# Attention with a gated MLP on one core: the first four pairs' scores from plain fp32 operands, and PSUM banks handed out per use

## The chip, the core and the metric

The kernel runs on one core of a Trainium2 chip. The core has TensorE (PE: matmuls, with a separate path for loading weights, PEld), VectorE (DVE), ScalarE (ACT) and GpSimd (POOL); SyncE (SP) issues all DMAs of this kernel. TensorE writes into PSUM, which the kernel uses as eight banks of 512 fp32 columns. The metric is device time in microseconds of one execution; the profile is of one execution on the chip.

## The reference

There are 8 batches of 8 heads, 576 positions, head size 64. Queries and keys are rotated, scores are softmaxed, values are weighted; the eight heads side by side (512 columns) are the input of a gated MLP with a spatial mix.

```python
q_rot, k_rot = (rotate(q), rotate(k))
scores = scale * np.matmul(q_rot, k_rot.transpose(0, 1, 3, 2))
scores = scores - np.max(scores, axis=-1, keepdims=True)
attn = np.exp(scores)
attn = attn / (np.sum(attn, axis=-1, keepdims=True) + 1e-09)
x = np.matmul(attn, v)                 # heads side by side: (8, 576, 512)
h = np.maximum(x @ w_in, 0.0)          # w_in 512 x 1024
u, v = h[..., :512], h[..., 512:]
v_n = (v - mu) / np.sqrt(var + 1e-06)  # mean and variance over the 512 columns
v_s = np.einsum('ts,bsd->btd', w_spatial, v_n) + b_spatial[None, :, None]
out = (u * v_s) @ w_out                # w_out 512 x 512
```

## The kernel before, in words

**Pairs.** Two heads of a batch form a pair: head 0 in partitions 0 to 63, head 1 in 64 to 127, positions along the columns. There are 32 pairs, numbered through; pairs 0 to 3 are batch 0. A pair's scores are nine tiles of 128 queries by 576 keys: tiles (0,0) to (0,3) of head 0, (1,0) to (1,3) of head 1, and (0,4), the last 64 queries of both heads. A score tile takes a place of two PSUM banks (288 keys in each); names `sc` in the profile.

**Two ways to score.** Pair 0 scores from plain fp32 operands (`mm_whole` in `scores`, L650): a tile of head h takes the 64 rows of that head, two matmuls, and each fp32 matmul stands as two passes in the trace. Pairs 1 to 31 score in fp32r (L641). There the operands are split into a high and a low part, and `prepare` copies them with ten DMAs into stacks of 128 rows (`qs`, `ks`, `lks`, one set for each head): a tile is four matmuls of 128 rows, tile (0,4) six. The split costs two roundings of whole tiles (L449 and L320) and two corners (`qt`) on ACT, one pass on DVE (L425, the low part of q) and one on POOL (L323, `lk`). The rotation itself is POOL's: two products and a sum each for q and k (L433, L437). The stacks exist once, so the next pair's copies wait for the last tile that reads them.

**After a tile.** DVE takes the row maxima (L661, `nmx`), ACT the exponential with its sum (L663, `et`), and then the place is free. In pairs 0 to 3 (`attention_plain`) TensorE transposes the exponentials in groups of three (L533, L536, `tp`), ACT or DVE copies the group out (L542, L544, `turns`), and TensorE multiplies with the values (L573, `pv`). From pair 4 on DVE transposes (L665) and TensorE multiplies in 32-row pieces (L603, `pvl`, `pvu`). `normalise` sends the sums through DRAM (`rt`, `rb`) and multiplies (L694).

**MLP.** Once the four pairs of a batch are normalised, `mlp` runs four sets of products: `pa` (L728), `pb` (L751), `pc` (L769), `pd` (L784). Between them and the pairs of the next batch TensorE alternates. The MLP's weights arrive as raw 64-bit numbers and are decoded once, in twelve blocks of 512 columns (`decode`, six passes on DVE and two on ACT a block, in a PSUM bank of their own).

**What sets the order.** No order is written out. Each step is an `op` with an engine, an assumed duration, a priority key (20 a pair, `K_...` constants as offsets) and what it reads and writes. `Program.run` plays the ops through with these durations: whenever an engine is free it takes the ready op with the lowest key whose buffers it can get, and that fixes each engine's order. The numbers of buffers are in `SLOTS`. In PSUM there are two places for score tiles (`sc`, banks 0 to 3) and four single banks (`pm`) for everything else: transposes, values, decode, MLP.

## Time and profile before

| | |
|---|---|
| median of 3 runs | 881.13 us (874.3, 881.13, 881.17) |
| profiled execution | 876.26 us, its span 874.5 us |
| mean granted clock of TensorE | 0.994 |
| busy: PE, DVE, ACT, POOL | 824.3, 602.2, 517.2, 512.0 us |
| DMA | 150.82 MB, 172 GB/s over the span |
| first score matmul, first MLP product | 9.2 us, 110.4 us |

A row of a group in the profile gives the line, the engine, the operation, output and inputs by name and shape, the count, busy time and mean duration, and the engine's idle time before these instructions with what ended it. A row of the timeline or of the chain begins with the start and the length in us. A row of a window gives for each engine the busy time in it, the granted clock of TensorE and the DMA's share and rate. TensorE's busy time is an upper bound of its work, because matmuls are pipelined.

### The profile page before, as it was taken

The page shows a single profiled execution, that of the slowest core. Times are in us where ns is not written, and L with a number is a line of the kernel's source. Part 1 is how long each engine was busy: PE and PEld are TensorE (multiplying, and loading weights), DVE is VectorE, ACT ScalarE, POOL GpSimd, SP SyncE. Part 2 cuts the span into 40 slices and gives each one's busy share as a digit, 9 for nine tenths or more (in the row PEclk, how much of TensorE's full clock was granted, in tenths as well). Part 3 has the DMA queues.
Part 4 walks back from the last instruction along what each step waited for, and adds up shares of the span by engine and source line. Part 5 has one row for each costly group of instructions (what it writes and reads, how often), then busy time and mean ns, then how long its engine had stood idle before and what let it go on. Part 6 is the DMA issues. An engine that isn't in the chain of part 4 may idle for free.

```text
span 874.5 us, 30219 instructions
## 1 busy us (share of the span) xinstructions
PE 824.3 (94%) x12554; PEld 744.4 (85%) x12554; DVE 602.2 (69%) x1213; ACT 517.2 (59%) x1303; POOL 512.0 (59%) x433
## 2 busy tenths in 40 slices
PE   4988899899999999998999999998999989999998
PEld 2665578789899998898899998988899978999898
DVE  4688989686787767666787657766687648875230
ACT  2788768455675557554676547645576536754342
POOL 6577755673586657574477754675486735742221
PEclk9999989999999999999999999999999999999999
DMA  6767787757677786668877786668677667663101
GB/s 238 231 198 201 200 243 169 165 141 208 178 193 192 175 206 169 162 170 202 200 180 178 170 207 182 174 168 209 172 186 191 161 173 203 166 142 91 48 1 55
DMA packets 68171, 150.82 MB, mean 172 GB/s; under 512 B 14530, under 2 KB 14786, under 8 KB 68035
## 3 DMA queue, kind: packets, MB, share of 16 engines
q1 hardware_dynamic: 68034, 148.90, 65.8%
q8 instruction: 99, 1.62, 0.8%
q14 instruction: 38, 0.30, 0.1%
HBM read 93.55 MB, written 9.58 MB: 118 GB/s over the span
## 4 chain that ended last, share of the span: by engine, by line
PE 59%; POOL 12%; DVE 9%; DMA 8%; ACT 7%; issue 3%; SPq 1%; POOLq 0%; ACTq 0%; DVEq 0%
PE sc L641 10%; PE pa L728 9%; PE pvu L603 9%; PE pd L784 8%; PE pc L769 8%; PE pvl L603 6%; DMA qs<-st 5%; PE pb L751 4%; POOL st L433 3%; DVE nmx L661 3%; POOL lk L323 2%; ACT et L663 2%; PE pv L573 2%; POOL st L437 2%; POOL x L323 2%
## 5 line engine op out<-in xcount | busy, mean ns | idle before, releaser
L661 DVE TENSOR_REDUCE nmx<-sc 128x1 f32<-128x576 f32 x288 | 212.4, 746 | 121.6 <-PE sc L641 110.1
L663 ACT ACTIVATE et<-sc,nmx 128x576 f32<-128x576 f32 x288 | 212.0, 737 | 115.1 <-DVE nmx L661 114.4
L433 POOL TENSOR_TENSOR st<-st,tabs 128x576 f32<-128x576 f32 x124 | 175.4, 1432 | 111.0 <-DMA st<-in_qk_dram 66.2
L665 DVE STREAM_TRANSPOSE et<-et 128x576 f32<-128x576 f32 x252 | 191.5, 766 | 38.0 <-ACT et L663 36.2
L603 PE MATMUL pvl<-et,vr 32*64 32x160 f32 (+1 forms) x4032 | 155.3, 294 | 9.1 <-issue 6.3
L603 PEld LDWEIGHTS pvl<-et,vr 32*64 32x64 f32 x4032 | 137.7, 131 | 22.4 <-issue 16.9
L603 PE MATMUL pvu<-et,vr 32*64 32x128 f32 (+1 forms) x4032 | 152.8, 294 | 3.6 <-issue 2.6
L641 PE MATMUL sc<-ks,qs 128*128 128x288 f32 x620 | 135.1, 307 | 18.1 <-ACT et L663 8.8
L641 PEld LDWEIGHTS sc<-ks,qs 128*128 128x128 f32 x620 | 98.1, 188 | 38.7 <-ACT et L663 14.1
L603 PEld LDWEIGHTS pvu<-et,vr 32*64 32x64 f32 x4032 | 122.2, 130 | 5.2 <-issue 3.5
L769 PE MATMUL pc<-wsp,vn 128*128 128x288 f32 x768 | 121.3, 295 | 0.0
L784 PE MATMUL pd<-g,wo 128*128 128x288 f32 x768 | 119.2, 299 | 0.0
L728 PE MATMUL pa<-wi,x 128*128 128x512 f32 x448 | 118.7, 402 | 0.4 <-DVE wi L323 0.3
L751 PE MATMUL pb<-x,wi 128*128 128x288 f32 x768 | 117.2, 296 | 0.6 <-DVE x L621 0.6
L751 PEld LDWEIGHTS pb<-x,wi 128*128 128x128 f32 x768 | 107.7, 188 | 3.6 <-issue 1.2
L784 PEld LDWEIGHTS pd<-g,wo 128*128 128x128 f32 x768 | 107.8, 190 | 2.5 <-issue 2.5
L769 PEld LDWEIGHTS pc<-wsp,vn 128*128 128x128 f32 x768 | 108.6, 188 | 0.3 <-DVE dcwo L364 0.2
L641 PE MATMUL sc<-lks,qs 128*128 128x288 f32 x496 | 106.2, 296 | 0.0
L728 PEld LDWEIGHTS pa<-wi,x 128*128 128x128 f32 x448 | 81.9, 192 | 16.2 <-issue 1.3
L323 POOL TENSOR_TENSOR vn<-vv,vn 128x512 fp32r<-128x512 f32 x32 | 41.2, 1290 | 88.6 <-ACT vn L320 84.8
L437 POOL TENSOR_TENSOR st<-st 128x576 f32<-128x576 f32 x62 | 89.2, 1439 | 3.8
L323 POOL TENSOR_TENSOR g<-u,g 128x288 fp32r<-128x288 f32 x64 | 54.2, 854 | 62.7 <-ACT g L320 62.7
(149 smaller groups left out, 1053.2 us busy)
## 6 DMA issues: line engine op xcount, KB each, us to landing
vr<-in_v_dram SPq DMA_DIRECT2D x116, 320.0 KB
st<-in_qk_dram SPq DMA_DIRECT2D x64, 576.0 KB
qs<-st SPq DMA_DIRECT2D x124, 144.0 KB
ks<-st SPq DMA_DIRECT2D x124, 144.0 KB
lks<-lk SPq DMA_DIRECT2D x62, 144.0 KB
out_dram<-ob SPq DMA_DIRECT2D x31, 288.0 KB
ws<-in_w_spT_dram SPq DMA_DIRECT2D x2, 576.0 KB
tabs<-in_tab_dram SPq DMA_DIRECT2D x1, 576.0 KB
```

The lines of the kernel that those rows point to most:

```text
L323: eng.tensor_tensor(out=lo, in0=src, in1=hi.bitcast(F32), op=ALU.subtract)
L433: f = lambda e: e.tensor_tensor(out=st[j][:, cols], in0=st[j][:, cols], in1=tabs[:, cols], op=ALU.mult)
L437: f = lambda e: e.tensor_tensor(out=st[j][:, :S], in0=st[j][:, :S], in1=st[j][:, S:2 * S], op=ALU.add)
L603: nc.tensor.matmul(bank(g)[64 * h:64 * h + 64, c0:c0 + 32 * (s1 - s0)], lhsT=vr[rows, b % 4, b // 4, h, :], rhs=et[rows, s0:s1, 32 * b:32 ...
L641: nc.tensor.matmul(pt[:, c * 512:c * 512 + HALF], lhsT=lhsT, rhs=rhs[:, c * HALF:(c + 1) * HALF], start=(n == 0), stop=(n == len(parts) - 1))
L661: op(DVE, 720, key + K_MAX, lambda: nc.vector.tensor_reduce(out=nmx.tile, in_=tops(), op=ALU.max, axis=AX.XY, negate=True), r=[pt], w=[nmx ...
L663: op(ACT, 880, key + K_EXP, lambda: nc.scalar.activation(et[:, at, :].rearrange("p (c n) -> p c n", c=2), tops(), AF.Exp, bias=nmx.tile, s ...
L665: op(DVE, 740, key + K_TURN, lambda: nc.vector.transpose(out=et[:, at, :], in_=et[:, at, :]), w=[(et, at)])
L728: nc.tensor.matmul(pm.tile, lhsT=lhsT, rhs=win[1, d][:, j, :], start=(d == 0 and n == 0), stop=(d == 3 and n == len(todo) - 1))
L751: nc.tensor.matmul(pm[:, :HALF], lhsT=win[0, d][:, i, f * P:(f + 1) * P], rhs=x[d][:, at:at + HALF], start=(d == 0 and n == 0), stop=(d == ...
L769: nc.tensor.matmul(pm[:, :HALF], lhsT=lhsT, rhs=rhs, start=(t == 0 and n == 0), stop=(t == 4 and n == 1))
L784: nc.tensor.matmul(pm[:, :HALF], lhsT=wout[d,][:, i, m * P:(m + 1) * P], rhs=gs[d][:, at:at + HALF], start=(d == 0 and n == 0), stop=(d == ...
```

## The change: what it does

1. Pairs 0 to 3 (`WHOLE` 1 to 4) score from plain fp32. `prepare_whole` for pairs 1 to 3: load, rotate and sum on POOL, one scaling of q by 1/8 on ACT; no split, no stacks.
2. `scores_whole` is one step for two tiles, t of head 0 and t of head 1: its matmuls go by half of the keys, and in each half head 0 and then head 1, in the two halves of the rows. It needs two score places at once (one for tile (0,4)). `RESERVE` keeps such a step's claim on places while it waits for them.
3. PSUM is one tile of eight banks. Banks are given out per use: a score tile takes two neighbouring banks from the bottom, within a limit of 4 tiles in pair 0, 3 in pairs 1 to 3, 2 later (`SCORE_SLOTS`, `limit`); single banks come from the top, 7 down to 4.
4. The stacks are opened late (`open_stacks`): their memory holds operands of pairs 0 and 1 first, and their zero fills run on POOL after pair 1 has scored.
5. A group of transposes waits only for the head whose exponentials it reads. Eight of the twelve weight decodes start only after the scores of pair 2, 3 or 4 (`GATE_U`, `GATE_O`).
6. Assumed durations are changed (DMAs with a rate of the wire, exponential 880 to 750 ns, maximum 720 to 680, decode 640 to 605), and the keys. `mlp(0)` is listed after pair 4 in place of pair 3.

```diff
-MOE_START, MOE_LENGTH = 90, 82
+MOE_START, MOE_LENGTH = 91.9, 82.99
...
-K_MAX, K_EXP, K_TURN, K_AV, K_COPY = 1.0, 2.0, 3.0, 24.0, 4.0
+K_MAX, K_EXP, K_TURN, K_AV, K_COPY = 1.55, 3.4, 2.08, 20.54, -3.71
...
-WHOLE = 1
+WHOLE = 4
+HOMES = [("stk", "stk"), ("stk", "stage"), ("stage", "stage"), ("xg", "xg")]
+RESERVE = True
+SCORE_SLOTS = [4, 3, 3, 3]
...
+        def vacant(pool, limit):
+            if pool not in PSUM:
+                return free[pool][0] if free[pool] else None
+            if pool == "pm":
+                return next((n for n in range(7, 3, -1) if banks[n] is None), None)
+            return next((n for n in range(limit) if banks[2 * n] is banks[2 * n + 1] is None), None)
...
+        opened = [t for a in range(2) for t in (("qs", a, 0), ("qs", a, 1), ("ks", a, 0), ("ks", a, 1), ("lks", a))]
+        op(POOL, 1800, 20 * WHOLE - 25, place, r=[("scored", i) for i in range(min(WHOLE, 2))], w=opened, new=wide)
...
+        else:
+            for j, st in ((1, k), (0, q)):
+                op(DMA, dma_ns(576), key - K_LOADW - j, lambda j=j, st=st: load(st.tile, qk[b, hp, j].rearrange("p c n -> p (c n)")), w=[(st, 0), (st, 1)], new=[st])
...
+            op(ACT, 573, key - K_HIQ, lambda: nc.scalar.activation(q[:, :S], q[:, :S], AF.Copy, scale=0.125), w=[(q, 0), (q, 1)])
...
+    def scores_whole(i, t, st, sm, et, key, new, turn):
+
+        q, k = st
+        pts = [Buf("sc", None, None, f"sc{i}_{a}_{t}") for a in range(2 if t < 4 else 1)]
+        for pt in pts:
+            pt.limit = SCORE_SLOTS[i]
+
+        def mm():
             for c in range(2):
+                for h in range(2):
                     own = slice(64 * h, 64 * h + 64)
                     q0 = t * P + TW * h if t < 4 else 4 * P * (1 - h)
+                    pt, rows = (pts[h], slice(0, P)) if t < 4 else (pts[0], own)
+                    nc.tensor.matmul(pt[rows, c * 512:c * 512 + HALF], lhsT=q[own, q0:q0 + rows.stop - rows.start], rhs=k[own, c * HALF:(c + 1) * HALF], start=True, stop=True)
...
+        o = op(PE, 1150, key, mm, r=[*need, *([] if new else [(et, "first")])], w=[*pts, *done, *([(et, "first")] if new else [])], new=[*pts, *new])
+        o.reserve = RESERVE
```

How the instructions move is shown at three places of TensorE's order. The first is the program's start. Before, pair 0's tiles of the two heads come one after the other (`sc0_h_t` is tile t of head h), and two groups of transposes stand ahead of the last:

```order
L650 MATMUL sc0_0_0_117<-st0_1_88,st0_0_103 128x288 x2
L650 MATMUL sc0_1_0_121<-st0_1_88,st0_0_103 128x288 x2
L650 MATMUL sc0_0_1_133<-st0_1_88,st0_0_103 128x288 x2
L650 MATMUL sc0_1_1_139<-st0_1_88,st0_0_103 128x288 x2
L650 MATMUL sc0_0_2_151<-st0_1_88,st0_0_103 128x288 x2
L650 MATMUL sc0_1_2_159<-st0_1_88,st0_0_103 128x288 x2
L650 MATMUL sc0_0_3_173<-st0_1_88,st0_0_103 128x288 x2
L650 MATMUL sc0_1_3_185<-st0_1_88,st0_0_103 128x288 x2
L533 MATMUL tp0_0_0a_193<-turns_83,et0_118 128x128 x3
L533 MATMUL tp0_0_0b_200<-turns_83,et0_118 128x128 x3
L650 MATMUL sc0_0_4_204<-st0_1_88,st0_0_103 64x288 x4
```

Now (L727 scores, L593 transposes, L633 values; all write the one PSUM tile):

```order
L727 MATMUL psum_63<-st0_1_83,st0_0_94 128x288 x16
L727 MATMUL psum_63<-st0_1_83,st0_0_94 64x288 x4
L593 MATMUL psum_63<-turns_78,et0_108 128x128 x15
L633 MATMUL psum_63<-turns_78,vr0_96 64x384 x2
L593 MATMUL psum_63<-turns_78,et0_108 128x128 x3
```

All nine tiles of pair 0 now stand ahead of its first transpose. The second place is pair 1's values with pair 2's scores. Before:

```order
L641 MATMUL sc2_1_1_612<-ks1_77,qs1_75 128x288 x2
L641 MATMUL sc2_1_1_612<-lks1_79,qs1_75 128x288 x2
L573 MATMUL pv1_1_578<-turns_83,vr1_128 64x192 x2
L641 MATMUL sc2_0_2_627<-ks0_76,qs0_74 128x288 x2
L641 MATMUL sc2_0_2_627<-lks0_78,qs0_74 128x288 x2
L573 MATMUL pv1_1_578<-turns_83,vr1_128 64x192
```

Now (`st2` is pair 2's operands, four matmuls are two tiles):

```order
L727 MATMUL psum_63<-st2_1_121,st2_0_134 128x288 x4
L593 MATMUL psum_63<-turns_78,et1_219 128x128 x6
L633 MATMUL psum_63<-turns_78,vr1_113 64x384 x2
L593 MATMUL psum_63<-turns_78,et1_219 128x128 x3
L633 MATMUL psum_63<-turns_78,vr1_113 64x192 x4
L593 MATMUL psum_63<-turns_78,et1_219 128x128 x3
L727 MATMUL psum_63<-st2_1_121,st2_0_134 128x288 x4
```

Single tiles among transposes and values have become steps of two tiles with more of the other work between them. The third place is what stands ahead of the first MLP product (L728, now L810). Before:

```order
L573 MATMUL pv3_1_1087<-turns_83,vr3_420 64x128
L641 MATMUL sc4_1_1_1169<-ks1_77,qs1_75 128x288 x2
L641 MATMUL sc4_1_1_1169<-lks1_79,qs1_75 128x288 x2
L641 MATMUL sc4_1_2_1176<-ks1_77,qs1_75 128x288 x2
L641 MATMUL sc4_1_2_1176<-lks1_79,qs1_75 128x288 x2
L641 MATMUL sc4_1_3_1197<-ks1_77,qs1_75 128x288 x2
L641 MATMUL sc4_1_3_1197<-lks1_79,qs1_75 128x288 x2
L728 MATMUL pa0_0_1205<-wi10_284,x0_467 128x512 x3
```

Now (`stk0` holds queries and keys of head 0, `stk1` of head 1, `stk2` the low parts of the keys):

```order
L633 MATMUL psum_63<-turns_78,vr3_344 64x128
L706 MATMUL psum_63<-stk1_453 128x288 x2
L706 MATMUL psum_63<-stk2_454,stk1_453 128x288 x2
L706 MATMUL psum_63<-stk0_452 128x288 x2
L706 MATMUL psum_63<-stk2_454,stk0_452 128x288 x2
L706 MATMUL psum_63<-stk0_452 128x288 x2
L706 MATMUL psum_63<-stk2_454,stk0_452 128x288 x2
L706 MATMUL psum_63<-stk0_452 128x288 x2
L706 MATMUL psum_63<-stk2_454,stk0_452 128x288 x2
L810 MATMUL psum_63<-wi10_325,x0_400 128x512 x6
```

Four tiles stand there in place of three, and three of them belong to pair 5. In the batches that follow, the products and the pairs' steps alternate in much the same way as before.

More of the change, by code (lines that the diff above doesn't have):

```diff
@@ L33 @@
 LATE = 1500
+KIB_NS = 3.6
+AHEAD = 1633
 FETCH = 2500
@@ L152, in place @@
             for b in bufs:
-                pool = next((p for n, p in enumerate(b.pools) if free[p] and not (n and own[p])), None)
+                pool = next((p for n, p in enumerate(b.pools) if vacant(p, b.limit) is not None and not (n and own[p])), None)
                 if pool is None:
                     for t in taken:
-                        free[t.pool].insert(0, t.slot)
+                        occupy(t, None)
                     return False
-                b.pool, b.slot = pool, free[pool].pop(0)
+                b.pool, b.slot = pool, vacant(pool, b.limit)
+                occupy(b, b)
                 taken.append(b)
@@ L641, in mm @@
                     nc.tensor.matmul(pt[:, c * 512:c * 512 + HALF], lhsT=lhsT, rhs=rhs[:, c * HALF:(c + 1) * HALF], start=(n == 0), stop=(n == len(parts) - 1))
-        def mm_whole():
+        heads = [a] if t < 4 else [0, 1]
+        need = [("qs", h, j) for h in heads for j in range(2)] + [("ks", h, j) for h in heads for j in range(2)] + ([("lks", a)] if t < 4 else [lk, "qt"])
+        done = [("scored", i)] if (a, t) == TILES[-1] else []
+        op(PE, 4 * pe_ns(HALF) if t < 4 else 6 * pe_ns(HALF), key, mm, r=[*need, *([] if new else [(et, "first")])], w=[pt, *done, *([(et, "first")] if new else [])], new=[pt, *new])
@@ L660, in scores @@
-        op(PE, 8 * pe_ns(HALF) if i < WHOLE else 4 * pe_ns(HALF) if t < 4 else 6 * pe_ns(HALF), key, mm_whole if i < WHOLE else mm, r=[*need, *([] if new else [(et, "first")])], w=[pt, *([(et, "first")] if new else [])], new=[pt, *new])
-        op(DVE, 720, key + K_MAX, lambda: nc.vector.tensor_reduce(out=nmx.tile, in_=tops(), op=ALU.max, axis=AX.XY, negate=True), r=[pt], w=[nmx], new=[nmx])
+        op(DVE, 680, key + K_MAX, lambda: nc.vector.tensor_reduce(out=nmx.tile, in_=tops(), op=ALU.max, axis=AX.XY, negate=True), r=[pt], w=[nmx], new=[nmx])
```

206 lines of the change are left out of this document (123 added, 83 removed).

## The prediction

> **What bounds the kernel now.** I read the page first (busy shares, slices), then the windows by stage, then the chain and the timeline of the first 110 us, then who waited for whom there.
>
> ```profile
> PE 824.3 (94%) x12554; PEld 744.4 (85%) x12554; DVE 602.2 (69%) x1213; ACT 517.2 (59%) x1303; POOL 512.0 (59%) x433
> ```
>
> TensorE is busy for 94% of the span, so what counts is when it gets work and what that work costs. The windows part the run: the plain stage (28.43 to 110.4; the first MLP product starts at 110.4 us), the first 5 us of the MLP, one MLP batch.
>
> ```profile
> core 0: us, PE busy (x) PEld busy (x) DVE busy (x) ACT busy (x) POOL busy (x), PEclk, DMA share, GB/s
> 28.43:47.30 18.87, 18.87 (x139) 13.02 (x138) 13.04 (x22) 15.79 (x39) 9.41 (x7) 1.00 0.60 201
> 47.30:68.20 20.90, 18.45 (x141) 12.69 (x140) 17.23 (x29) 16.83 (x42) 15.72 (x13) 1.00 0.73 207
> 68.20:88.80 20.60, 18.38 (x135) 11.96 (x135) 16.77 (x30) 17.20 (x43) 15.22 (x12) 1.00 0.75 218
> 88.80:110.40 21.60, 17.79 (x132) 12.30 (x130) 20.80 (x36) 16.88 (x44) 15.31 (x13) 0.96 0.80 193
> sum 81.97, PE 73.48 PEld 49.98 DVE 67.84 ACT 66.71 POOL 55.67; mean PE 18.37 PEld 12.49 DVE 16.96 ACT 16.68 POOL 13.92
> ...
> 110.40:115.40 5.00, 5.00 (x13) 3.94 (x13) 3.49 (x7) 2.32 (x7) 4.71 (x4) 0.51 1.04 273
> ...
> 218.50:317.80 99.30, 97.35 (x1666) 90.73 (x1666) 72.21 (x147) 60.33 (x155) 65.26 (x54) 1.00 0.74 186
> ```
>
> Each pair of the plain stage takes 19 to 22 us, of which TensorE works 18 to 19: it is the bound there, with 81.97 - 73.48 = 8.5 us idle, and DVE is next (20.80 of 21.60 in the last window). An MLP batch takes about 100 us with 2 us of idle. So a saving is worth its face value only if it brings the first MLP product forward, or takes idle time from the batches. Ahead of the plain stage lie the scores of pair 0, told by the chain and by the timeline of TensorE:
>
> ```profile
> 9.16 2.30 PE sc L650 x8
> 11.48 0.77 DVE nmx L661
> 12.29 0.05 issue
> 12.34 0.84 ACT et L663 x2
> 13.18 0.04 issue
> 13.22 2.30 PE sc L650 x6
> ...
> 13.22 3.01 PE L650 MATMUL sc<-st,st 64*128 64x288 f32 x8 [1.77 <-ACT et L663]
> 17.22 3.07 PE L650 MATMUL sc<-st,st 64*128 64x288 f32 x8 [0.99 <-ACT et L663]
> 21.29 3.62 PE L650 MATMUL sc<-st,st 64*128 64x288 f32 x8 [1.00 <-ACT et L663]
> 24.84 0.90 PE L533 MATMUL tp_0a<-turns,et 128*128 128x128 f32 x3
> 25.54 0.84 PE L533 MATMUL tp_0b<-turns,et 128*128 128x128 f32 x3
> 26.31 2.19 PE L650 MATMUL sc<-st,st 64*64 64x288 f32 x8
> ```
>
> Two tiles start together, and the next two wait until the exponentials of these are done and their banks free: a round of 4 us (9.16, 13.22, 17.22, 21.29), of which TensorE works 2.3. The ninth tile ends at 28.5 us.
>
> **The change, part by part.** *Pair 0's scores.* By the order, five operations (two tiles each, the last one tile) now stand ahead of the first transpose, with four tile places. The first two need no place of another: 9.16 + 2.30 = 11.5 us, and about 13.5 us. The third needs the first one's places: exponentials at 12.34 + 0.84 and once more, 14.0 us, so it ends at 16.0. The fourth waits for the exponentials of the second (maxima from 13.5, exponentials done by 16.0) and ends at 18. The fifth, one tile, ends at about 20. The two transposes that stood before the ninth tile (0.90 + 0.84, overlapping: 1.5 us) come after, so that the point reached at 28.5 is reached at 21.5: **-7**. Its bounds: the nine exponentials alone, 12.34 + 9 x 0.84 = 19.9, would allow -8.5; one more wait for a place, 1 us as in the row of 17.22, leaves -6.
>
> By the Trainium skill (TensorE: Matmul & The Clock Gate, What's actually happening) TensorE leaves its half clock after some 3.4 us of sustained work; here the first transposes at 24.84 still ran slow though TensorE had worked with 1 us gaps since 9.16, and with the gaps closed the third to fifth operation would by that rule run at half their time, which makes the sum below about 866 in place of 867.
>
> *The work of pairs 1 to 3.* What a score tile costs stands in the chain, cold and warm:
>
> ```profile
> 24.91 0.83 PE tp_0a L533 x3
> 25.74 0.64 PE tp_0b L533 x3
> ...
> 32.86 0.33 PE tp_3b L533 x3
> ...
> 54.54 0.52 PE sc L641 x4
> ...
> 57.66 0.72 PE sc L641 x4
> ...
> 88.15 0.79 PE sc L641 x6
> ```
>
> The same transposes take 0.64 us early and 0.33 later, so early TensorE runs at half speed and a two-tile operation of 2.30 us should be 1.15 warm. Its two heads already run side by side before: eight passes in 2.30 us (and in 2.19, 64 columns) are four passes' time. A pair then costs 5 x 1.15 = 5.8 us. The stacked form costs 0.52 a tile behind a transpose and 0.72 behind a value product, eight times, and 0.79: 5.0 to 6.6. Equal within a microsecond, three times: 0, from -2.5 to +2.5. The half-row shape differs from that of the transposes, where the stacked tile had the same; counted in the order up to the first MLP product, TensorE changes shape 86 times, 76 before. At 0.72 - 0.52 = 0.2 each that is +2; some fall into idle time: **+1**.
>
> *Waits in the plain stage.* Of its idle time nearly all is one kind:
>
> ```profile
> PE sc L641 <- ACT et L663: 6.3, 6, 1.8
> PE tp L536 <- ACT turns L542: 1.2, 1, 1.2
> PE tp_2a L533 <- DVE turns L544: 0.9, 2, 0.6
> ```
>
> A tile waits for its place. The old order put three to six tiles in a row behind each other; the new one spreads the five operations of a pair over the values of the pair before, though four tiles in a row still stand ahead of the first MLP product. But an operation now takes both places at once. Behind a waiting operation stand all transposes and values of the order, and DVE and ACT wait for those. I take half of the 6.3 us away, **-3**; bounds -6.3 (all goes) and +8 (as much idle again).
>
> *What pairs 1 to 3 no longer need.* Per pair: ten copies of 144 KB, two roundings and two corners on ACT, one pass each on DVE and POOL; one scaling on ACT comes in.
>
> ```profile
> L323 POOL TENSOR_TENSOR lk<-st 128x576 fp32r<-128x576 f32 x31 | 44.3, 1430 | 9.5 <-ACT st L320 8.5 <-ACT et L663 0.4
> L425 DVE SCALAR_TENSOR_TENSOR st<-st 128x576 fp32r<-128x576 f32 x31 | 28.1, 906 | 3.3 <-ACT st L449 3.3
> L449 ACT ACTIVATE st<-st 128x576 fp32r<-128x576 f32 x31 | 21.1, 682 | 12.6 <-POOL st L437 11.2 <-DMA ks<-st 1.4
> L320 ACT ACTIVATE st<-st 128x576 fp32r<-128x576 f32 x31 | 21.0, 676 | 2.6 <-POOL st L437 2.6
> L320 ACT ACTIVATE qt<-st 64x64 fp32r<-64x64 f32 x62 | 15.6, 251 | 2.0 <-PE sc L641 1.6
> ```
>
> POOL loses 3 x 1.43 = 4.3 us, DVE 3 x 0.91 = 2.7, ACT 3 x (0.68 + 2 x 0.25) = 3.5, the queues 30 x 144 KB = 4.3 MB. None of it ends the stage while TensorE has work in front of it: 0; if DVE decides at its end, -2.7. The stacks' fills move from the start to pair 4's preparation on POOL, whose load was 55.67 of 81.97 us: hidden; without that cover some 1 us. The gate on the last eight weight decodes only orders DVE's work; it doesn't change its amount.
>
> *Behind the first product.* The clock of 0.51 in the window from 110.4 costs 5 x 0.49 = 2.4 us. It follows idle time at the end of the stage, and the row of four tiles there is as long: 0, bound -2.4. In the batches the same work stands in nearly the same order with other times; what may change is this wait in 218 to 818 us:
>
> ```profile
> PE sc L641 <- DMA qs<-st: 7.3, 8, 1.7
> ```
>
> I take 0: all of it gone would be -7, as much again +7; for a range half of each is enough, since the copies keep their number and their queue.
>
> Three tiles of pair 5 now stand ahead of the first product, 3 x 0.52 = 1.6 us that are moved and not added.
>
> **The sum.** -7 + 1 - 3 = -9, against the profiled execution's own 876.26 us (span 874.5 and 1.8 around it): 867. The median of the runs shown is 881.13, and one of three lies at 874.3, so the runs part by 0.8%; the profiled one is 4.9 us below the median, and the range has to hold a time that falls on the upper of these.
>
> **The rivals.** *More comes off (-20, 856).* All 6.3 us of waits go (-3.3 more), the clock at the first product stays up (-2.4), and half of the copies' waits and some of DVE's load go (-5). For it: the maxima and exponentials of two tiles are now costed nearer to the rows. Against it: three independent things. 0.17.
>
> *DVE takes it back (-2, 874).* In the last window of the stage DVE worked 20.80 of 21.60 us. Its work up to pair 4's last maximum is the same in both orders, but for 2.7 us. TensorE may come earlier and wait for DVE. Against it: DVE idled 28.43 to 47.3 for 5.8 us and before that for the scores of pair 0, and these times are what closes. 0.17.
>
> *Slower: the round of two places.* Outside pair 0 almost every two-tile operation takes the same two places, so each waits for both exponentials of the one before: TensorE 1.15, maximum 0.77, two exponentials 0.84 each and 0.2 of hops make 3.8 us, no more than the 18.37 / 5 = 3.7 us of TensorE's work per operation. But every transpose's copy that ACT or DVE does in between lengthens it, and 16.8 to 17.2 us of ACT's work a pair leave little room. Over some 14 rounds the gain is gone at 3.7 + 9 / 14 = 4.35 us; at 5.1, the cold round of 4.06 with one more microsecond in it, the stage is 14 x 1.4 = 19.6 us longer: -7 + 1 + 19.6 = +13.6, 890. For it: before, a tile waited for one exponential only. Against it: pair 0's round of 4.06 held 2.30 of cold TensorE. 0.14.
>
> That the two heads don't overlap when issued in turn would cost 0.96 more in 15 operations; the rows of 2.30 and 2.19 us speak against it, and it is counted into the last case.
>
> **How the numbers follow.** The forecast, 867, has 0.52, its own range 861 to 873. The range of 854 to 881 leaves out most of the slow case and the end of the fast one. A difference of 1% (about 8.8 us) is what a measurement of this kernel can tell from none. Faster: 0.17, and three fifths of the forecast's cases, 0.48. Within 1%: the rest of the forecast's and DVE's case, 0.38. Slower: 0.14.
>
> **What would show it.** Pair 0's last score matmul ends near 20 us; pair 1 to 3's operations take 1.1 to 1.2 us each with both heads' passes side by side; the first MLP product starts at 101 to 104 us in place of 110.4; the batches behind take 100 us as before. Wrong would be: rounds above 4.3 us with TensorE waiting for exponentials in pairs 1 to 3; a first product before 104 us whose batch then takes longer than before; or batches that differ by over 1 us each.

## The result, and the profile after

The changed kernel takes 849.89 us in the median of its runs (846.92 to 854.35), the kernel before 881.15 beside it: a ratio of 0.968, with an interval of 0.964 to 0.972. That is 31 us less, below the predicted range of 854 to 881. The two profiled executions lie 21.9 us apart (spans of 874.5 and 852.6), because the one of before lies at the low end of its kernel's times and the one after, 854.35 us and so just inside the range, is the longest of its own; the terms below are read from these two.

The page of the changed kernel:

```profile
PE 817.7 (96%) x12560; PEld 735.4 (86%) x12560; DVE 600.2 (70%) x1210; ACT 510.1 (60%) x1294; POOL 505.4 (59%) x430
```

TensorE works 7 us less than before and idles some 15 us less. The windows tell where. They show the changed kernel from its first transpose to the first MLP product, the first 5 us behind that, batch 0, batches 1 to 6 and the tail; a batch runs from its first product to that of the next.

```profile
core 0: us, PE busy (x) PEld busy (x) DVE busy (x) ACT busy (x) POOL busy (x), PEclk, DMA share, GB/s
18.77:101.30 82.53, 76.77 (x563) 45.91 (x563) 72.20 (x123) 69.00 (x173) 63.18 (x52) 1.00 0.61 183
101.30:106.30 5.00, 5.00 (x17) 3.95 (x16) 5.00 (x10) 2.14 (x5) 0.26 (x1) 0.66 1.06 213
101.30:203.60 102.30, 98.61 (x1648) 91.05 (x1647) 83.66 (x168) 61.57 (x154) 62.55 (x53) 0.97 0.72 178
203.60:795.80 592.20, 580.49 (x9954) 542.88 (x9954) 421.04 (x861) 351.64 (x902) 356.36 (x295) 0.99 0.70 177
795.80:852.60 56.80, 53.67 (x362) 50.81 (x360) 13.04 (x46) 21.17 (x51) 12.71 (x14) 1.00 0.07 27
```

And the same three last stretches of the kernel before:

```profile
110.40:218.50 108.10, 100.94 (x1658) 92.36 (x1658) 85.74 (x173) 64.89 (x160) 62.56 (x52) 0.98 0.72 185
218.50:817.70 599.20, 580.89 (x9956) 542.12 (x9956) 422.91 (x864) 353.52 (x905) 362.02 (x298) 1.00 0.71 176
817.70:874.50 56.80, 53.52 (x361) 50.77 (x360) 13.05 (x46) 21.73 (x53) 13.23 (x14) 1.00 0.07 27
```

The first MLP product comes at 101.3 in place of 110.4 us (-9.1), batch 0 takes 102.3 in place of 108.1 (-5.8), batches 1 to 6 592.2 in place of 599.2 (-7.0), the tail is the same. In batches 1 to 6 TensorE's work is equal within 0.4 us; it is idle time that went, 18.3 us before and 11.7 after. In batch 0 it is not equal: 98.6 us in place of 100.9, and 1.6 of these 2.3 us are the three tiles of pair 5 that now run ahead of the batch.

The start, by TensorE's timeline (start, duration, what, how often, idle time ahead of it):

```profile
9.90 3.69 PE L727 MATMUL psum<-st,st 64*128 64x288 f32 x16 [9.90 <-DVE st L547]
13.96 4.52 PE L727 MATMUL psum<-st,st 64*128 64x288 f32 x24 [0.38 <-ACT et L745]
18.77 1.83 PE L593 MATMUL psum<-turns,et 128*128 128x128 f32 x15 [0.29 <-ACT et L745]
...
23.41 1.24 PE L727 MATMUL psum<-st,st 64*128 64x288 f32 x8
```

All of pair 0's scores are done at 18.5 us, with one pause of 0.38; the first operation of pair 1, warm (its passes at the fast pace), takes 1.24 us. TensorE's waits are listed next (who waited for whom: us in total, times, longest), first those of scores up to the first MLP product, then those in batches 1 to 6. `issue` is idle time in which TensorE waited for nothing that the profile shows.

```profile
PE psum L706 <- ACT et L745: 2.3, 3, 1.5
PE psum L727 <- ACT et L745: 0.4, 1, 0.4
```

```profile
PE psum L662 <- issue: 8.1, 7, 1.7
...
PE psum L706 <- DMA stk<-st: 0.3, 1, 0.3
```

The 7.3 us for which a score tile waited for its stack copies are 0.3 now.

### The profile page after: what moved, and what is told of

It is laid out like the page before. It is cut to its first block, busy times and chain, and to the rows that moved or that the text cites. A ratio compares the mean times of both kernels' runs of the same rounds, so it can differ in the third digit from the quotient of the medians.

```text
span 852.6 us, 30090 instructions
## 1 busy us (share of the span) xinstructions
PE 817.7 (96%) x12560; PEld 735.4 (86%) x12560; DVE 600.2 (70%) x1210; ACT 510.1 (60%) x1294; POOL 505.4 (59%) x430
## 4 chain that ended last, share of the span: by engine, by line
PE 81%; DMA 6%; ACT 4%; DVE 3%; issue 2%; POOL 1%; SPq 1%; POOLq 0%; ACTq 0%; DVEq 0%
PE psum L662 16%; PE psum L706 15%; PE psum L851 13%; PE psum L866 12%; PE psum L810 12%; PE psum L833 8%; DMA stk<-st 3%; DMA st<-in_qk_dram 3%; ACT et L745 2%; PE psum L633 1%; PE psum L593 1%; PE psum L727 1%; SPq L370 1%; DVE et L747 1%; DVE nmx L743 1%
## 5 line engine op out<-in xcount | busy, mean ns | idle before, releaser
L745 ACT ACTIVATE et<-psum,nmx 128x576 f32<-128x576 f32 x288 | 212.8, 740 | 76.5 <-DVE nmx L743 75.7
L743 DVE TENSOR_REDUCE nmx<-psum 128x1 f32<-128x576 f32 x288 | 212.8, 746 | 59.3 <-PE psum L706 50.2
L662 PE MATMUL psum<-et,vr 32*64 32x160 f32 (+1 forms) x8064 | 156.1, 295 | 9.2 <-issue 9.0
L662 PEld LDWEIGHTS psum<-et,vr 32*64 32x64 f32 x8064 | 138.9, 131 | 22.6 <-issue 18.2
L833 PE MATMUL psum<-x,wi 128*128 128x288 f32 x768 | 121.7, 299 | 4.7 <-ACT u L836 3.5
L851 PE MATMUL psum<-wsp,vn 128*128 128x288 f32 x768 | 125.5, 298 | 0.0
L706 PE MATMUL psum<-stk 128*128 128x288 f32 x560 | 118.7, 301 | 3.6 <-ACT et L745 2.3
L866 PE MATMUL psum<-g,wo 128*128 128x288 f32 x768 | 119.5, 297 | 0.0
L810 PE MATMUL psum<-wi,x 128*128 128x512 f32 x448 | 118.9, 401 | 0.1
L851 PEld LDWEIGHTS psum<-wsp,vn 128*128 128x128 f32 x768 | 109.9, 190 | 3.9 <-issue 3.9
L810 PEld LDWEIGHTS psum<-wi,x 128*128 128x128 f32 x448 | 80.9, 190 | 15.2 <-issue 1.4
```

Source lines behind the costliest of these rows:

```text
L662: nc.tensor.matmul(bank(g)[64 * h:64 * h + 64, c0:c0 + 32 * (s1 - s0)], lhsT=vr[rows, b % 4, b // 4, h, :], rhs=et[rows, s0:s1, 32 * b:32 ...
L706: nc.tensor.matmul(pt[:, c * 512:c * 512 + HALF], lhsT=lhsT, rhs=rhs[:, c * HALF:(c + 1) * HALF], start=(n == 0), stop=(n == len(parts) - 1))
L743: op(DVE, 680, key + K_MAX, lambda: nc.vector.tensor_reduce(out=nmx.tile, in_=tops(), op=ALU.max, axis=AX.XY, negate=True), r=[pt], w=[nmx ...
L745: op(ACT, 750, key + K_EXP, lambda: nc.scalar.activation(et[:, at, :].rearrange("p (c n) -> p c n", c=2), tops(), AF.Exp, bias=nmx.tile, s ...
L810: nc.tensor.matmul(pm.tile, lhsT=lhsT, rhs=win[1, d][:, j, :], start=(d == 0 and n == 0), stop=(d == 3 and n == len(todo) - 1))
L833: nc.tensor.matmul(pm[:, :HALF], lhsT=win[0, d][:, i, f * P:(f + 1) * P], rhs=x[d][:, at:at + HALF], start=(d == 0 and n == 0), stop=(d == ...
```

## The experiments

Two things were to be explained: why the batches, whose work is the same but for the 2.3 us in batch 0, gained 12.8 us; and whether the 9.1 us ahead of them came from the places or from the form of the scores. The "numbers" below are the constants, keys and due times, from which the planner makes the order; when they or the operations change, it plans every engine's order anew. The table has all kernels that ran: when the first product of batch 0 and that of batch 1 start, how long batches 1 to 6 take (all three from the profiled execution, which for one kernel differs by up to 1% from the next), and the ratio to the kernel before on the same chip with its interval (there the median of the kernel before was 877 to 882 us). In e17 144 small matmuls of pair 4's values stand ahead of the first MLP product; the first product of batch 1 is the better mark there.

| kernel | batch 0 at | batch 1 at | batches 1 to 6 | ratio |
|---|---|---|---|---|
| before | 110.4 | 218.5 | 599.2 | 1 |
| changed | 101.3 | 203.6 | 592.2 | 0.968 (0.964 to 0.972) |
| e1 stacked pairs 1 to 3 | 111.0 | 217.3 | 607.6 | 0.997 (0.994 to 1.000) |
| e2 old numbers | 104.4 | 205.6 | 606.5 | 0.989 (0.986 to 0.993) |
| e3 two places | 110.5 | 217.9 | 603.2 | 0.998 (0.994 to 1.001) |
| e4 before, new numbers | 113.6 | 222.8 | 602.9 | 1.010 (1.006 to 1.013) |
| e5 two places, changed order from pair 4 on | 114.1 | 216.0 | 588.1 | 0.981 (0.977 to 0.985) |
| e6 changed, e3's order from pair 4 on | 111.9 | 214.9 | 604.5 | 1.000 (0.997 to 1.003) |
| e7 changed order, two places | 115.1 | 216.6 | 583.7 | 0.986 (0.982 to 0.991) |
| e8 four places, then two | 104.1 | 210.6 | 596.9 | 0.992 (0.989 to 0.995) |
| e9 e3, TensorE's row changed | 112.4 | 216.1 | 583.8 | 0.982 (0.976 to 0.987) |
| e10 e3, transfers' row changed | 110.7 | 212.1 | 602.8 | 0.996 (0.993 to 0.999) |
| e11 before, values behind copies | 109.2 | 219.2 | 642.5 | 1.039 (1.032 to 1.045) |
| e12 e1, changed order from pair 4 on | 125.9 | 224.2 | 587.0 | 0.989 (0.984 to 0.994) |
| e13 before, seven tiles later | 109.7 | 217.5 | 610.4 | 1.000 (0.997 to 1.002) |
| e14 changed again | 100.9 | 203.3 | 589.6 | 0.964 (0.960 to 0.967) |
| e15 four places, stacked, old numbers | 116.8 | 224.4 | 605.4 | 1.007 (1.003 to 1.011) |
| e16 two places, unstacked, old numbers | 112.8 | 219.8 | 600.2 | 0.997 (0.993 to 1.000) |
| e17 before, four places | 117.9 | 214.0 | 594.2 | 0.989 (0.983 to 0.995) |
| e18 before, TensorE's row changed | 110.6 | 224.5 | 604.2 | 1.006 (1.003 to 1.008) |

### One part undone at a time

**e1: pairs 1 to 3 stacked again.**

```diff
-WHOLE = 4
+WHOLE = 1
```

> The changed kernel with pairs 1 to 3 scored in the stacked form again; pair 0 unstacked with four places, all the new numbers, and the banks per use stay. After the change the first MLP product came 9.1 us earlier and the batches behind it took 12.8 us less. Theory A (the batches' gain comes from the new numbers that set the order, whatever the form of the scores): the first product comes at 101 to 106 us, the batches keep their 12.8 us, the time is 850 to 858. Theory B (the batches gain because pairs 1 to 3 need no copies, no roundings and no corners, so that the first MLP batch starts with less left to do): batch 0 loses its 5.8 us, the rest of the batches their 7, and the time is 863 to 872.

Neither theory had it: the batches lost their gain, and so did the stage ahead of them, although pair 0's scores ended as early as in the changed kernel. The windows of that stage, and two pieces of the chain of waits through it:

```profile
20.60:40.00 19.40, 15.95 (x108) 9.54 (x108) 13.98 (x19) 13.35 (x33) 15.08 (x12) 0.91 0.70 196
40.00:60.00 20.00, 17.73 (x129) 11.86 (x129) 18.92 (x31) 17.28 (x43) 10.54 (x9) 1.00 0.82 234
60.00:80.00 20.00, 17.78 (x119) 11.18 (x116) 17.12 (x31) 15.32 (x41) 14.87 (x12) 0.91 0.93 283
80.00:111.00 31.00, 25.83 (x185) 18.17 (x182) 28.10 (x47) 22.46 (x58) 22.68 (x19) 0.91 0.75 190
```

```profile
20.36 2.97 DVE st L478
...
45.64 6.68 DMA stk<-lk
```

From 20.6 to 111.0 us TensorE works 77.3 of 90.4 us. What now stands in the chain is what the stacked form needs and the unstacked one doesn't: the low part of pair 1's queries on DVE, 2.97 us long, ahead of a copy that TensorE waits for, and a stack copy of 6.68 us. (The low part takes 0.75 us in the median of its 31 times; this once, POOL worked from 19.96 to 22.71.) The transfers' share rises to 0.93. Of TensorE's own waits, though, the longest is the old one, for exponentials (6.3 us before); ahead of stack copies it waits only 0.5 us:

```profile
PE psum L706 <- ACT et L745: 6.8, 8, 1.7
PE psum L633 <- DVE turns L604: 3.1, 2, 2.4
```

So the stacked work stands in the chain, but that it alone keeps the product at 111.0 is not shown: the order was planned anew, too.

**e2: the old table of numbers.**

```diff
-DEC_U = [61.8, 94.8, 112.1, 106.0]
-K_MAX, K_EXP, K_TURN, K_AV, K_COPY = 1.55, 3.4, 2.08, 20.54, -3.71
+DEC_U = [65, 98, 107, 104]
+K_MAX, K_EXP, K_TURN, K_AV, K_COPY = 1.0, 2.0, 3.0, 24.0, 4.0
...
```

> The changed kernel with the table of numbers of the kernel before (due times of the decodes and of every step); the form of the scores, the banks, the assumed durations and the transfer model of the planner stay as changed. Theory A (the new numbers carry the batches' gain): the first product still comes near 101 us, perhaps a few us later, but the batches take their old 108 and 100 us each; time 862 to 870. Theory B (the form carries it): the batches stay at 102 and 99 us; time 849 to 856.

Theory A holds for batches 1 to 6, which lose 14.3 us; the stage loses 3, and the time, 870.28 us, lies at A's upper edge. Batch 0 keeps its gain (101.2 us), as B had it. The lost time is not in waits for copies (1.9 us in batches 1 to 6) but put down to issue (13.1 ahead of value products).

**e3: two places throughout.**

```diff
-SCORE_SLOTS = [4, 3, 3, 3]
+SCORE_SLOTS = [2, 2, 2, 2]
```

> The changed kernel with two score tiles at a time from the start on, where it has four for pair 0 and three for pairs 1 to 3. My prediction put the third two-tile operation of pair 0 at the end of the first round only with two places, and took 1 us for each wait for a place: with two places four rounds of about 4 us stand at the start, as before, so that the first product comes 4 to 6 us later and the time is 854 to 856. Rival: the time lost at the start is idle time that DVE and ACT need anyway before the first MLP product; the first product comes less than 1.5 us later and the time is 849 to 851.

Both missed: the first product is 9.2 us later, and the batches behind it, which take two places in either kernel, 16 us longer. A number that concerns pairs 0 to 3 alone alters the plan of everything behind them. In batches 1 to 6 of e3 the old wait is back:

```profile
PE psum L706 <- DMA stk<-st: 7.5, 5, 2.0
PE psum L662 <- issue: 6.5, 7, 1.4
PE psum L706 <- ACT et L745: 2.9, 6, 1.1
```

**e4: the new numbers in the kernel before.** The same lines as in e2, the other way round, in the kernel before.

> The kernel before with the new table of numbers (due times of the decodes and steps) and nothing else of the change; its planner still assumes the old durations and transfers. Theory A (the new numbers carry the batches' gain by themselves): the first product stays near 110 us, the batches gain up to 12.8 us, time 866 to 872. Theory B (the form carries it) and theory C (the numbers help only together with the new durations and the new transfer model, against which they were set): no gain, 876 to 886 or later.

Theory B or C: 886.65 us, a loss of 1%. So the numbers are worth nothing by themselves; e1 and e3 say that with the new numbers, too, the gain is gone when the form or the places are missing.

**e8: four places for pair 0, two for the rest.**

```diff
-SCORE_SLOTS = [4, 3, 3, 3]
+SCORE_SLOTS = [4, 2, 2, 2]
```

> Four places for pair 0 as changed, two for pairs 1 to 3 where the change has three; planned freely with the new numbers. In the changed kernel only two operations of pairs 1 to 3 took the third place (the last tile of pairs 2 and 3). Theory A (the places of pairs 1 to 3 change nothing themselves, and the new numbers fit only the list that they were set for): the first product at 101 to 104 us, batches 703 to 712 us, time 860 to 872. Theory B (the third place does nothing and the order hardly moves): time 849 to 855.

Theory A, at its upper end: 870.23 us. Only two operations took the third place, yet without it the plan comes out another way: batch 1 starts 7.0 us later, and batches 1 to 6 take 4.7 us more.

### The order by itself

These runs write the order out: each engine's list of operations is recorded from one kernel and imposed on another; what isn't in the list is planned freely. In the kernels the lists are packed into one string; where a cut below shows a row, it gives the operations by name.

```diff
+ORDER = (
...
+)
...
-                    if item[2].eng:
+                    if item[2].eng or set_by_row.get(item[2], e) != e:
                         continue
+                    if item[2] in set_by_row and item[2] is not row[e][0]:
+                        passed.append(item)
+                        continue
```

**e5, e6: stage and order exchanged.**

> Two score places from the start on, as in e3, but everything that belongs to pair 4 and later (scores, values, all MLP batches, their loads and copies) is issued on each engine in the order of the changed kernel, which is written out; the stage of pairs 0 to 3 is planned freely. In e3 the first product came at 110.5 us and the seven batches from it to the eighth first product took 710.6 us, against 101.3 and 694.5 in the changed kernel. Theory A (the batches' gain lies in their order alone): batches 693 to 699 us, the stage near 110, time 860 to 866. Theory B (a late or crowded start disturbs the batches behind it): batches 705 to 715 us, time 872 or more.

> The changed kernel's four and three places, but everything of pair 4 and later is issued in the order that the kernel with two places (e3) had. Theory A (the batches' gain lies in their order): the first product comes at 101 to 104 us and the batches take 706 to 714 us, time 866 to 874. Theory B (the early start makes the batches shorter): batches 693 to 699 us, time 850 to 856.

The windows of batches 1 to 6, of e5:

```profile
216.00:804.10 588.10, 578.27 (x9956) 541.07 (x9955) 421.31 (x861) 351.37 (x902) 356.26 (x295) 1.00 0.71 179
```

and of e6, with its longest wait there (L819 is the stacked scores; written-out orders shift the lines):

```profile
214.90:819.40 604.50, 582.56 (x9948) 542.72 (x9948) 415.74 (x860) 350.29 (x902) 355.33 (x295) 0.99 0.68 174
```

```profile
PE psum L819 <- DMA stk<-st: 10.4, 6, 2.1
```

Theory A holds in both directions for the batches: with a late stage and the changed order they are shorter still than in the changed kernel (e5 takes 857.64 us), with e3's order they take 604.5 behind four and three places. The stage of e6 was not early, though (111.9 for 101 to 104 expected), perhaps because pair 4's loads and tiles stand in it, in e3's order. So e6 shows the order's price and not what the early stage gives alone; for that, e2 and e8 have a first product at 104 us and batches 1 to 6 of 606.5 and 596.9. An early start by itself doesn't shorten them. And the order does not explain batch 0: it takes 103.0 us in e6 and 101.2 in e2, without the changed order, and 101.9 in e5 with it.

**e7: the changed order whole, but two places.**

> The whole order of the changed kernel on every engine, but only two score tiles at a time in PSUM. It tells the places apart from the order that the planner makes with them. By my prediction's steps the places matter for pair 0 alone, where the second to fourth operation then wait for the exponentials of the one before: three rounds of 4 us in place of 8.6 us for five operations, first product at 105 to 108 us, and the batches at 693 to 699 us: time 854 to 860. Rival: nothing else in the order is late for it, because DVE and ACT need the time anyway; first product at 101 to 103 us, time 850 to 853.

Batches 1 to 6 take 583.7 us, the shortest of all. The first product comes at 115.1, 13.8 us later, more than either expected. TensorE's waits up to there:

```profile
PE psum L850 <- DVE st L670: 9.1, 1, 9.1
PE psum L850 <- ACT et L868: 8.2, 6, 1.8
```

The unstacked operations (L850) wait 8.2 us for exponentials, where the changed kernel waits 0.4. Of the 8.2, 5.0 are four waits within pair 0's scores, which end at 27.5 us in place of 18.5; the other two (1.6 and 1.7) stand ahead of the last tiles of pairs 2 and 3. The two-tile operations of pairs 1 to 3 do not wait for exponentials.

**e9, e10: one row alone.** As e3, with the changed kernel's row of pair 4 and later on one engine.

> As e3 (two places from the start on), but of pair 4 and later TensorE's instructions alone stand in the changed kernel's order; the other engines and the transfers are planned freely around it. In e5, with every engine's order taken over, the first product came at 114.1 us, the batches took 690.0 us and the time was 857.6; in e3 110.5, 710.6 and 877. Theory A1 (TensorE's own order of scores, values and products carries the batches' gain): batches 688 to 696 us, time 858 to 864. Theory A2 (the order of the transfers carries it, by having the stacks copied in time): batches 703 to 712 us, time 870 to 878.

> As e9, but the transfers of pair 4 and later alone stand in the changed kernel's order. Theory A1 (TensorE's order carries the gain): batches 703 to 712 us, time 870 to 878. Theory A2 (the order of the transfers carries it): batches 688 to 696 us and the waits for stacks, 7.5 us in e3, under 2; time 858 to 864.

Batches 1 to 6 of e9, and TensorE's waits in them:

```profile
216.10:799.90 583.80, 577.39 (x9955) 539.50 (x9954) 418.61 (x861) 351.37 (x903) 355.89 (x296) 1.00 0.71 180
```

```profile
PE psum L705 <- issue: 4.1, 5, 1.6
PE psum L876 <- ACT u L879: 1.2, 5, 0.3
PE psum L749 <- DMA stk<-st: 0.5, 2, 0.3
```

and of e10:

```profile
PE psum L731 <- DMA stk<-st: 6.4, 4, 2.1
```

TensorE's row carries the gain (583.8 us, the waits for copies nearly gone, the time 863.89); the transfers' row doesn't (602.8, the waits still 6.4, 873.54).

**e12: stacked pairs 1 to 3, changed order from pair 4 on.**

> Pairs 1 to 3 in the stacked form as in e1, but everything of pair 4 and later in the changed kernel's order on every engine. In e1 the first product came at 111.0 us and the batches took 713.9. If the batches' gain lies in the order alone, they take 686 to 696 us here too and the first product stays at 111 to 116: time 856 to 866, so that most of the whole gain is had without the change of form. If the stacked stage itself disturbs the batches: batches over 700 us, time 870 or more.

The batches follow the order again (587.0). The stage doesn't keep its 111 us: the first product comes at 125.9 and batch 1 starts at 224.2, perhaps because pair 4's early steps stand in an order made for an unstacked stage. The time, 869.42 us, lies outside both expectations.

### The waits for copies, the suspect

**e11: the values' load behind the copies.** In the kernel before, each of the loads moves past five copies in the transfers' row; the rest of the order is its own.

```diff
-vr8, qs9, ks9, ks9, lks9, qs9
+qs9, ks9, ks9, lks9, qs9, vr8
```

> The kernel before in its own order on every engine; the one thing moved is the load of the values of a pair (1.28 MB), which stood just ahead of the first five stack copies of the next pair in the transfer queue and now stands just behind them, for pairs 5 to 30. Before, TensorE waited 7.3 us for stack copies in eight places. Theory (the copies land late because the values' load moves ahead of them): these waits fall under 2 us, the time by 4 to 7 us to about 872. Rival (the load then comes late for the value products, or the copies are late for their inputs): as much is lost again, the time is 876 or more.

The rival, and far beyond it: 914.16 us. The waits for copies are gone from the list, and in batches 1 to 6 there stands in their place:

```profile
PE pvu L728 <- DMA vr<-in_v_dram: 15.6, 18, 1.6
PE pvu L728 <- issue: 7.6, 7, 2.6
PE sc L766 <- ACT et L788: 6.9, 8, 1.4
```

So the load did hold the copies up. By the Trainium skill (DMA: Bandwidth & Descriptors, Queues, rings and completion order) a DMA engine takes its descriptors in ring order; the trace agrees, since what is moved forward lands in time and what is moved back is late. Moved behind all five copies, the load comes late for the value products and costs more than the waits did.

**e13: the first tile later.** In the kernel before, TensorE's row alone is altered, for the seven pairs that waited longest.

```diff
-sc12, pd, pd
+pd, sc12, pd
```

> The kernel before in its own order on every engine; the one thing moved is the first score tile of pairs 12, 16, 20, 23, 24, 28 and 31 (those that waited longest for their stack copies, 0.97 to 1.96 us), which stands one product of the MLP later in TensorE's row. Theory A3 (in the changed order the first tile of a pair comes late enough for its copies, and that is the gain): TensorE's waits for copies fall from 7.3 to under 3 us, the batches by 4 to 6 us, time 871 to 874 where before is 877. Rival (the wait for copies only covers another one behind it, for the exponentials and the weights' products; the gain is in the whole arrangement): the waits for copies fall and others take their place, the batches stay within 2 us.

The rival, by the time: no difference (ratio 1.000). Batches 1 to 6 did not stay within 2 us, though; they took 610.4 in this profile, the longest of its kernel's executions. The waits there:

```profile
PE pvl L727 <- issue: 8.4, 7, 2.3
PE sc L765 <- DMA qs<-st: 4.6, 6, 1.2
PE pvu L727 <- issue: 3.6, 2, 2.9
PE sc L765 <- ACT sums L812: 3.0, 4, 0.8
```

2.7 of the 7.3 us of waits for copies went, less than the theory asked for; 3.0 us for ACT's sums and more time put down to issue came.

**e18: TensorE's row in the kernel before.** From pair 5 on, planned around with the old numbers.

> The kernel before, with TensorE's instructions of pair 5 and later in the changed kernel's order, and the other engines and the transfers planned around it with the old numbers; nothing else of the change. In e9 TensorE's row brought batches of 687.5 us where the free plan had 710.6. If TensorE's order is enough by itself, the batches take 686 to 696 us here and the time falls to 860 to 870 although no form and no place is altered; if it needs the new numbers on the other engines, the batches stay over 703 us and the time is 874 or more.

No gain: batches 1 to 6 take 604.2 us. The waits for copies are down here too (7.3 before); for exponentials they are up (0.9 before):

```profile
PE sc L681 <- ACT et L703: 9.7, 7, 1.7
...
PE sc L681 <- DMA qs<-st: 1.6, 4, 0.8
```

Here TensorE's row didn't get its exponentials in time, in e9 it did. Which part brings them is not shown, since e18 lacks the new numbers, but also the new form, the new assumed durations and the new model of transfers.

### The places and the form

**e15, e16: one part each, with the old numbers.** The constants of e1 and e3, and the table of e2.

> Four places for pair 0, pairs 1 to 3 stacked, and the table of numbers of the kernel before: my prediction's first term alone, -7 us, against the kernel before. By the prediction the first product comes at 103 to 104 us and the time is 868 to 872. By what e1 showed with the new numbers (the copies, roundings and turns of the stacked pairs decide as soon as the start is earlier) the first product comes at 108 to 112 us and the time is 874 or more.

> Pairs 1 to 3 unstacked with two score places throughout, and the table of numbers of the kernel before: the prediction's second and third terms alone, +1 and -3 us. By the prediction the first product comes at 107 to 109 us, time 873 to 876. By e3 (110.5 us with the new numbers) there is no gain without the places: 110 to 112 us, 876 to 880.

Neither comes out as the prediction had it: 116.8 and 112.8 us for the first product, 889.03 and 879.28 us in all. The shares of the chain of waits of e15, from 9 us to that product:

```profile
by line: PE psum L706 15.4%; SPq L370 10.2%; DMA stk<-lk 8.4%; ACT et L745 8.2%; issue 8.0%; DMA st<-in_qk_dram 6.7%; PE psum L633 6.7%; DVE nmx L743 6.2%; DMA vr<-in_v_dram 5.2%; POOL st L486 5.2%; PE psum L593 4.7%; DMA wi12raw<-in_w_in_d
```

Transfers and the queue that issues them hold over a third of it. But e15 also has the changed kernel's assumed durations, for which the old numbers weren't set; e17 leaves these out.

**e17: the places alone, in the kernel before.**

```diff
         pt = Buf("sc", None, None, f"sc{i}_{a}_{t}")
+        pt.limit = 4 if i == 0 else 2
```

(With it `vacant`, `occupy` and the one PSUM tile of the change.)

> The kernel before with PSUM banks given out per use and four score places for pair 0; nothing else of the change (one tile per operation, old numbers, old durations, stacked pairs 1 to 3). By the prediction's first term pair 0's scores end near 20 us and the first product comes at 103 to 105 us, batches as before: time 870 to 874. By e1 and e15 the stacked pairs behind it take the gain back: pair 0's scores end near 20 us all the same, the first product comes at 108 to 112 us, time 876 to 882.

869.51 us, close to what the prediction's first term gives (876.26 - 7), but by luck: the kernel before had a median of 881.88 beside it, and the term is 7 us at the start and nothing behind it. Pair 0's scores end at 19.8 us, 8.7 earlier than before; of that 4.5 us are left at the start of batch 1 (the mark of 117.9 has pair 4's value products ahead of it), and 5.0 came off batches 1 to 6 in this profile. Pair 0's scores, and batches 1 to 6:

```profile
9.30 10.48 PE L672 MATMUL psum<-st,st 64*128 64x288 f32 x40 [9.30 <-DVE st L515]
```

```profile
214.00:808.20 594.20, 577.81 (x9956) 540.17 (x9955) 421.03 (x864) 353.85 (x904) 361.48 (x298) 1.00 0.72 178
```

With places enough, one tile per operation takes 10.48 us for the forty passes; two heads in turn take 3.69 + 4.52. That is not shown to be the form's doing: e17's passes stayed slow for longer. They are listed with 684 ns or more up to 16.6 us and with 402 from 17.8 on, where the changed kernel has 684 or more up to 12.0 and 403 from 12.9; while slow, mostly two passes start every 0.48 us in either kernel.

By the start of batch 1, the four places alone bring 4.5 us (e17) or, planned with the new numbers, 1.2 (e1); the form alone 0.6 (e3), or -1.3 with the old numbers (e16); both together 12.9 (e2) and 14.9 (changed). (e15, 5.9 us later than before, plans the old numbers with the new durations, which may be what spoils it.) Each of these kernels has a plan of its own, and a plan is worth several us: the form with two places brings 6.4 with another row for the transfers (e10), and both parts bring 3.6 with pair 4's steps in e3's order (e6). So both together bring more than their sum only in some plans, and what the parts are worth apart from the plan is not shown.

**e14: the changed kernel once more.**

> The changed kernel once more, unaltered. First product at 101 to 102 us, batches 685 to 695 us, ratio 0.965 to 0.972. In e5, e7 and e9 the same order of TensorE gave batches of 690.0, 685.2 and 687.5 us, against 694.5 in the first profile of the changed kernel: if they are 685 to 690 here, the first profile was a slow one in its idle time that is put down to issue (10.0 us there, 5 to 8 in the others).

As expected within 0.1 us in the stage and 0.001 in the ratio (0.964); batches 1 to 6 take 589.6 us, between the first profile and e7, and batch 0 102.4. The idle time put down to issue is 8.0 us ahead of value products again, so that the 4 us by which e9 is faster in it stay unexplained. No other kernel that ran is faster than the changed one.

## Why the prediction was wrong, by its own steps

**Pair 0's scores, -7: right, and 2 us too small.** The scores end at 18.5 us (forecast: near 20), and six transposes of the fifteen that follow at 18.77 are through at 18.77 + 6/15 x 1.83 = 19.5, where the forecast had 21.5 and before 28.5. The mis-sized piece is the 2.30 us of a two-tile operation: the first two took 3.69 together and the last 24 passes 4.52, 0.19 us each, against 0.29 before and 0.155 warm (1.24 for 8). The passes got fast at 12.9 us, 3.0 after the first one. By the Trainium skill (TensorE: Matmul & The Clock Gate, What's actually happening) TensorE leaves its half clock after some 3.4 us of sustained work; the changed kernel comes near that, but in e17, where TensorE worked without a pause from 9.30 us, the passes stayed slow for over 7 us, and in e14 for about 5 (403 ns from 14.3, the first at 9.13). In these runs the time is not a fixed one.

**Work of pairs 1 to 3, +1: right within a microsecond.** TensorE's work from the first transpose to the first MLP product is 76.77 us, 3.3 more than before. Of it 6/15 x 1.83 = 0.7 are the six transposes that stood ahead of this window before, and 1.6 the three tiles of pair 5 that moved there. The rest is 1.0. An operation takes 1.24 us, for 1.15 forecast. The three tiles were rightly called moved and not added: they make the first product 1.6 us later and batch 0 as much shorter.

**Waits in the plain stage, -3: right.** Idle time in that window went from 8.5 to 82.53 - 76.77 = 5.8 us; what stacked tiles wait for exponentials there went from 6.3 to 2.3.

**What pairs 1 to 3 no longer need, 0: wrong as a reason, though the sum came out.** It was put at nothing since TensorE had work ahead of it. With the early start of e1 that fails: TensorE idles 13.1 of 90.4 us there. The stacked work remains: copies and low parts stand in the chain, pauses slow the clock, and the first product stays at 111.0. (Waits for exponentials, 6.8 us, and a new plan are in that number too, so the share of the copies is argued and not shown.) By the start of batch 1, no kernel that ran without the form gained more than 4.5 us; in the changed kernel it is 14.9.

**Behind the first product, 0: the step that failed.** It rested on the sentence that the batches hold the same work in nearly the same order, and its bounds were -2.4 and -7. The two profiles differ by 12.8 us there, 5.8 in batch 0 and 7.0 in batches 1 to 6. (The medians differ by 9 us more than the profiles; in which stage is not shown.) In batches 1 to 6 the work is the same (580.5 and 580.9 us); the order was not near enough. Every kernel with the changed kernel's order of pair 4 and later on TensorE, with the new numbers for the other engines, takes 583.7 to 592.2 us for batches 1 to 6 (changed, e5, e7, e9, e12, e14); every other one 594.2 or more, whatever stage lies ahead of it. These are single profiles, and some lie up to 8 us from their kernel's median; with that difference taken off, an estimate that puts all of it into these batches, the two groups are 583 to 589 and 596 or more. TensorE's idle time there is 6.4 to 11.7 us in the first group and 16.0 or more in the second. TensorE's row alone is enough in the new plan (e9); in the kernel before, with old numbers, form and durations, it is not (e18). Of the two pieces that I had priced, the cold clock behind the first product gave 5 x (0.66 - 0.51) = 0.75 us; and the 7.3 us of waits for copies did go, but their going is not the gain by itself: 2.7 us of them taken away brought no gain (e13), all of them taken away by moving the load brought a loss (e11), and in e2 and e18 they are below 2 us in batches no shorter than before. What in TensorE's row makes the difference, beyond these waits, stays open. So does batch 0, whose 5.8 us are the 1.6 of the moved tiles, 0.75 of the clock and 3.5 us of idle time that no run explains; batch 0 is as short in kernels without the changed order (e2, e6, e10).

**The rivals.** *More comes off* had the size (-20 against the -21.9 of the profiles) by luck, with other pieces: not all waits of the stage, not 2.4 us of clock, but more of the batches. It had 0.17 because it was read as three independent things; that one plan moves them together was left out. *DVE takes it back*: DVE worked 72.2 of 82.5 us, and TensorE's waits for it in the stage came to little. *The round of two places*: TensorE waited 0.4 us for exponentials ahead of unstacked operations, so that the round did not lengthen. Two places throughout, in the same order (e7), cost 13.8 us at the first product, but most of that is pair 0, whose scores end 9.0 us later; the two-tile operations of pairs 1 to 3, which the rival of 890 was about, don't wait even there. Only the last tiles of pairs 2 and 3 do, 3.2 us together.

**What would show it**: pair 0's end, the operations' duration (a little above) and the first product before 104 us came as listed; batches that differ by over 1 us each were listed as wrong, and the first is 5.8 us shorter, the next six 7.0 together.

## What to carry to other kernels

Where a planner sets the order from a table, a change to one stage is a change to all of it: the batches behind deserve a term with bounds of their own, and a table set for one list of operations says little for another one (e1, e3 and e8 keep at most 7 of the 31 us, and e4 gains nothing). To learn what a change is worth, impose the recorded order of one kernel on the other, row by row; that told the order from the places and from the early start in e5, e7 and e9. And a wait in the profile is no price: before it is counted as a gain, ask what stands right behind it: here loads came late (e11) or sums did (e13) where the waits for copies had been.

## What was not expected of the hardware

In e1 TensorE paused 2.43 us for a copy on DVE and then ran slow for some 3.6 us:

```profile
20.56 0.87 PE L633 MATMUL psum<-turns,vr 128*64 128x384 f32 x4
23.85 1.55 PE L633 MATMUL psum<-turns,vr 128*64 128x384 f32 x4 [2.43 <-DVE turns L604]
25.33 2.23 PE L593 MATMUL psum<-turns,et 128*128 128x128 f32 x9
27.49 0.87 PE L633 MATMUL psum<-turns,vr 128*64 128x384 f32 x4
```

The same four products take 0.87 us ahead of the pause, 1.55 right behind it, and 0.87 again at 27.49. The granted clock from 20.60 to 40.00 us is 0.91. So this pause of 2.43 us cost nearly 2 us more than itself: 0.68 in the products, and 2.23 against 9/15 x 1.83 = 1.10 in the transposes. Shorter pauses need not: in batches 1 to 6 of the kernel before, where the longest wait is 1.7 us, the granted clock is 1.00. So idle time removed from TensorE can be worth more than its own length, as here, but is not always.
